# Splitting TensorE sets by columns so that a tile holds 2560 TensorE instructions, with a four-bank first dense layer and gate_w loaded by SyncE

## The chip, the core and the metric

The kernel runs on one core of a Trainium2 chip. The core has a matrix engine (TensorE, PE in the profile; its weight loads are listed as PEld), a vector engine (DVE), a scalar engine (ACT), GpSimd (POOL) and SyncE (SP), which issues most of the transfers, and 16 DMA engines. Every engine works through its own stream of instructions and waits for others by semaphores. The metric is the device time of one execution in microseconds (us); lower is better.

## The reference, cut to what matters

x is [1, 2048, 512]. Branch A walks through 64 segments of 32 tokens; each segment sees 8 memory tokens that the segment before it produced, so the segments form a chain. Branch B is a dense MLP over all 2048 tokens. A gate mixes them.

```python
def _A_ref(x, mem0, Wq, Wk, Wv, Wo, seg_len):      # M = 8, H = 32 heads, Dh = 128
    for s in range(n_seg):                          # 64
        h = concat([mem, x[:, s*32:(s+1)*32]], axis=1)
        q, k, v = h @ Wq, h @ Wk, h @ Wv            # per head
        p = softmax(mask(q @ k.T * Dh ** -0.5))
        o = (p @ v) @ Wo
        mem = o[:, :M]
        outs.append(o[:, M:])
b = gelu(layernorm(x) @ w1 + b1) @ w2 + b2          # 512 -> 1376 -> 512
g = sigmoid((x * gate_w).sum(-1, keepdims=True))
out = g * A(x) + (1 - g) * b
```

## The kernel before, in words

**Stages.** The first part (to about 75 us) computes the MLP. Eight blocks of 256 tokens run through `a_mm` (first dense layer, 11 chunks of up to 128 features; each chunk is four matmuls over 256 columns into a PSUM bank `hp`, then a Gelu on ACT) and `b_mm` (second layer, one matmul of 512 columns for the token tiles that aren't put off). Only even tiles up to 12 get their second layer here, in bank U[0] or U[2]; the hidden values of the others go to DRAM (`h_dr`) and are multiplied later as filler. Meanwhile SyncE loads 16 MB of attention weights. `gate_sums` on DVE multiplies x by `gw_bc`, which is gate_w copied to all 128 partitions.

The second part is the loop over 64 segments (L753 to L866). Four segments are a tile T (128 tokens); `si` is the segment's place in it. A segment does, in the order of the TensorE stream: the q and k projections (`qk_unit`, 64 matmuls of 512 columns), scores, the v projection (`v_unit`), softmax sums, probabilities times v (`av`, L290 and L295: 40 short matmuls), the output projection (`wo_pass`, which calls `wo_group` eight times), and `new_mem`, whose three parts turn the first 8 output rows into the next segment's memory. The chain from one segment to the next goes through `wo_pass`, copies on ACT and `new_mem`.

**Sets of four.** A matmul in this loop fills 32 rows of the output, and four of them stand side by side at column positions 0, 32, 64 and 96 of the array, so they run together. Such a set of four, over 512 columns, is one call of `qk_unit`, `v_unit` or `wo_group`. Every matmul has its own weight load before it, so a set is eight instructions.

**Filler.** `side(T, si)` gives a generator of work that isn't in the chain: projections of tokens left over for the next tile (si 0, 1, 3), `wo_left` for the tile before (si 2). `run(n)` takes n units of it. The lists `WS` say how many units go where: W1 after the v projection, W2 after `av`, W3 after `wo_pass`, then one unit after each of the first two `new_mem` parts. `next(mlp, None)` adds halves of the postponed MLP work.

**What sets the order.** All of it is a hand-written order (`manual_schedule`): each engine's stream is the order in which the Python code emits instructions. The TensorE stream is straight-line code, without loops, up to the rarely taken branch at the end. Counted in it, wait-only instructions included, a tile of the middle of the loop holds 2412 TensorE instructions: segments of 609, 601, 601 and 601.

Of the kernel before, what the change touches and what calls it, by code (L numbers as in the profile page):

```python
# [28 lines left out]
def kernel(ctx, tc, A_x, A_mem0, A_Wq, A_Wk, A_Wv, A_Wo, A_seg_len, B_x, B_w1, B_b1, B_w2, B_b2, gate_w, out):  # L29
    nc = tc.nc  # L30
    P = 128
# [4 lines left out]
    nseg = S // seg  # L36
# [86 lines left out]
    HF = ((0, H // 2), (H // 2, H))  # L123

    def qk_unit(bk, G, t, hf, kc):
        h0, h1 = HF[hf]
        for j in range(4):
            nc.tensor.matmul(bk[32 * j:32 * j + 32, :], lhsT=G[:, kc, :], rhs=W5[t][:, kc, h0:h1, j, :],  # L128
                             start=(kc == 0), stop=(kc == KC - 1), tile_position=(0, 32 * j))

# [14 lines left out]
    def v_unit(bk, G, vb, kc):  # L145
        for j in range(4):
            nc.tensor.matmul(bk[32 * j:32 * j + 32, :], lhsT=G[:, kc, :], rhs=Wv5[:, kc, 4 * vb:4 * vb + 4, j, :],  # L147
                             start=(kc == 0), stop=(kc == KC - 1), tile_position=(0, 32 * j))

# [4 lines left out]

    def wo_group(bk, U_, n):
        j, ih = HORD[n]
        for c in range(4):
            i = 4 * ih + c
            nc.tensor.matmul(bk[32 * c:32 * c + 32, :], lhsT=U_[:, j, i, :], rhs=Wo_sb[:, 4 * i + j, :],  # L159
                             start=(n == 0), stop=(n == NW - 1), tile_position=(0, 32 * c))  # L160

# [139 lines left out]
    with tc.tile_pool(name="mlpw", bufs=1) as mlpw, \  # L301
# [33 lines left out]
        def ld_w2(eng, a, b):  # L335
            eng.dma_start(w2_sb[:, a:b, :], B_w2[a * P:b * P, :].rearrange("(fc p) d -> p fc d", p=P))
# [6 lines left out]
        nc.sync.dma_start(w1_sb[:, :, F1:F], w1v[:, :, F1:F])  # L343
        nc.gpsimd.dma_start(gw_bc[:], gate_w.partition_broadcast(P))
        ld_w2(nc.sync, H2, H2 + 2)
        ld_w2(nc.sync, H2 + 2, FC - 1)
        nc.sync.dma_start(w2_sb[:FR, FC - 1, :], B_w2[(FC - 1) * P:F, :])
        nc.sync.dma_start(w2_sb[FR:FR + 1, FC - 1, :], B_b2.rearrange("(o d) -> o d", o=1))
# [128 lines left out]
        def a_mm(blk, fc):  # L477
            rows = min(P, F - fc * P)
            n = blk * FC + fc
            hp = (SbF, W, U[3], SbF)[n] if n < 4 else (W, SbF, U[2], U[3])[n % 4] if blk == NBLK - 1 else (W, SbF)[n % 2]  # L480
            for kc in range(KC):
                nc.tensor.matmul(hp[:rows, 0:TB * P], lhsT=w1_sb[:, kc, fc * P:fc * P + rows], rhs=yTs[blk][:, kc, :], start=(kc == 0), stop=(kc == KC - 1))  # L482
            nc.scalar.activation(out=hTm[blk % 2][:rows, :, fc, :], in_=hp[:rows, 0:TB * P].rearrange("p (t c) -> p t c", t=TB), func=ACTF.Gelu_apprx_tanh, bias=b1_sb[:rows, fc:fc + 1], scale=1.0)
# [128 lines left out]

    def run(n):
        for _ in range(n):
            next(fill, None)

    def chain(*gens):
# [113 lines left out]

    def wo_pass(U_, cuts=(0, Dm), bk=W):
        for n in range(NW):
            wo_group(bk, U_, n)
        w = cw.tile([P, Dm], BF16, tag="w", bufs=8, name="w")
        for a, b in zip(cuts, cuts[1:]):
            nc.scalar.copy(out=w[:, a:b], in_=bk[:, a:b])  # L737
        return w
# [10 lines left out]


    QK4 = ((0, 0), (1, 0), (0, 1), (1, 1))
    WS = ((2, 2, 1), (2, 2, 2), (2, 2, 2), (2, 2, 2))
    for s in range(nseg):  # L753
# [91 lines left out]
        prep_q(s + 1)  # L845
        w = wo_pass(UT[s % 2], (0, P, 2 * P, Dm), X2)
        if s >= 1:
            ws[s - 1] = w
        run(W3)
        if si:  # L850
# [3 lines left out]
        new_mem(w, hn, 0, si)  # L854
        run(1)
        new_mem(w, hn, 1, si)
        run(1)
        new_mem(w, hn, 2, si)
# [201 lines left out]
```

## Time and profile before

| | |
|---|---|
| median of 3 runs | 754.07 us (753.94 to 754.29) |
| the profiled execution's own time | 755.67 us |
| its span in the profile | 753.8 us |
| TensorE busy | 736.0 us (98%) |
| ScalarE busy | 535.6 us (71%) |
| VectorE busy | 399.5 us (53%) |
| GpSimd busy | 274.2 us (36%) |
| DMA engines busy, first four of 40 slices | 90% or more |
| DMA engines busy after that | 10 to 40% |

The profile has groups of instructions by line (how often, mean time of one, idle time before them and what ended it), a table of waits, the chain of work that ended last, a timeline, and a view of the DMA queues. A wait that is put down to "issue" is time in which an engine waited for nothing that the profile shows. Matmuls are pipelined: a matmul is shown from its start to a modelled end that lies well behind the start of the next, so small gaps between starts do not show as idle time; differences between starts do.

### The profile page before, as it was taken

The numbers are of one execution on the slowest core, as the hardware profiler recorded it, in microseconds if no ns is written. First come the engines' busy times: TensorE is split into PE (matmuls) and PEld (weight loads), VectorE is DVE, ScalarE is ACT, GpSimd is POOL, SyncE is SP. The second block draws the span as 40 slices with busy tenths as digits, with TensorE's granted clock in tenths as the row PEclk, the third lists the DMA queues.
The fourth block names the chain that finished last, engine by engine and source line by source line (L and its number), as shares of the span: only waits on it lengthen the run. The fifth ranks groups of instructions, "written<-read, shape, count | busy, mean of one in ns | idle before, by whom it ended". The sixth has DMA issues, their size and how long they took to land.

```text
span 753.8 us, 45384 instructions
## 1 busy us (share of the span) xinstructions
PE 736.0 (98%) x19896; PEld 429.8 (57%) x19896; DVE 399.5 (53%) x1415; ACT 535.6 (71%) x1627; POOL 274.2 (36%) x516
## 2 busy tenths in 40 slices
PE   8999999999999999999999999999999999999996
PEld 5776555555555555555555565555555655555553
DVE  6776555446454554445554545445464545555444
ACT  5777667777776776777777777767777777777663
POOL 4001323444324444334433344333443334433341
PEclk9999999999999999999999999999999999999999
DMA  9999323122321323221322313231323222222321
GB/s 312 343 335 362 104 85 87 55 76 72 93 77 46 91 70 96 69 83 53 92 77 80 86 46 93 68 96 67 70 72 86 79 72 78 57 90 74 95 70 37
DMA packets 69997, 77.17 MB, mean 102 GB/s; under 512 B 34873, under 2 KB 59938, under 8 KB 68258
## 3 DMA queue, kind: packets, MB, share of 16 engines
q1 hardware_dynamic: 68802, 72.65, 31.4%
q8 instruction: 157, 2.57, 1.4%
q0 software_dynamic: 448, 1.05, 0.5%
q10 hardware_dynamic: 544, 0.52, 0.3%
q14 instruction: 46, 0.38, 0.2%
HBM read 60.21 MB, written 7.70 MB: 90 GB/s over the span
## 4 chain that ended last, share of the span: by engine, by line
PE 91%; DVE 3%; DMA 2%; issue 2%; ACT 1%; POOL 0%; DVEq 0%; SPq 0%; ACTq 0%; POOLq 0%
PE U L128 33%; PE X L159 19%; PE X L147 17%; PE X L128 4%; PE U L290 3%; PE W L674 3%; PE U L147 2%; PE SbF L482 1%; PE U L266 1%; DMA xt<-in_A_x_dram 1%; PE W L482 1%; PE U L489 1%; DVE junk L465 1%; PE SbF L266 1%; PE SbF L701 1%
## 5 line engine op out<-in xcount | busy, mean ns | idle before, releaser
L730 POOL TENSOR_TENSOR UT<-XR,Rb 128x384 bf16<-128x384 bf16 x126 | 140.2, 1134 | 310.1 <-DMA Rb<-r_dr 252.6
L133 ACT CAST Tb<-U 128x512 bf16<-128x512 f32 x288 | 168.7, 586 | 78.7 <-PE U L128 72.5
L128 PEld LDWEIGHTS <-hT 128*32 128x32 bf16 x4096 | 108.9, 96 | 95.5 <-DVE hT L748 1.1
L147 PE MATMUL X<-Wv_sb,hT 128*32 128x512 bf16 x2048 | 144.9, 378 | 0.9 <-issue 0.9
L128 PE MATMUL U<-Wq_sb,hT 128*32 128x512 bf16 x2048 | 145.1, 380 | 0.0
L128 PE MATMUL U<-Wk_sb,hT 128*32 128x512 bf16 x2048 | 144.6, 379 | 0.0
L159 PE MATMUL X<-Wo_sb,UT 128*32 128x512 bf16 x2016 | 123.0, 380 | 0.2
L748 DVE CAST hT<-U 128x8 bf16<-128x8 f32 x126 | 21.0, 167 | 172.0 <-PE U L746 131.1
L811 ACT CAST V<-X 128x256 bf16<-128x256 f32 x256 | 88.7, 372 | 16.4 <-PE X L147 3.5
L137 DVE STREAM_TRANSPOSE QT<-Tb 128x256 f32<-128x256 f32 x128 | 57.0, 446 | 71.9 <-ACT Tb L133 71.5
L159 PEld LDWEIGHTS <-UT 128*32 128x32 bf16 x2048 | 56.6, 96 | 57.1 <-issue 17.7
L707 ACT CAST XR<-U 128x256 bf16<-128x256 f32 x252 | 78.6, 438 | 0.0
L737 ACT CAST w<-X 128x128 bf16<-128x128 f32 x189 | 44.8, 310 | 45.8 <-PE X L159 45.1
L137 DVE STREAM_TRANSPOSE KT<-Tb 128x256 f32<-128x256 f32 x128 | 57.0, 445 | 25.3 <-ACT Tb L133 25.3
L730 POOL TENSOR_TENSOR UL<-XR,Rb 128x128 bf16<-128x128 bf16 x126 | 60.2, 500 | 0.0
L147 PEld LDWEIGHTS <-hT 128*32 128x32 bf16 x2048 | 47.0, 94 | 22.3 <-issue 1.8
L842 ACT CAST UT<-U 128x64 bf16<-128x64 f32 x252 | 35.3, 227 | 28.2 <-PE U L295 28.2
L722 POOL TENSOR_TENSOR racc<-racc,R 128x72 f32<-128x72 f32 x63 | 21.2, 337 | 93.6 <-DVE R L720 49.9
L674 PE MATMUL W<-w_sb,hm 128*32 128x256 bf16 x728 | 52.7, 273 | 0.1
L794 ACT ACTIVATE E<-U 128x64 bf16<-128x64 f32 (+1 forms) x128 | 35.0, 273 | 11.3 <-PE U L270 11.1
L482 PEld LDWEIGHTS <-w_sb 128*128 128x128 bf16 (+1 forms) x352 | 33.5, 100 | 13.4 <-issue 2.4
L159 PE MATMUL X<-Wo_sb,UL 128*32 128x512 bf16 x512 | 39.8, 379 | 0.2 <-issue 0.2
(178 smaller groups left out, 1223.0 us busy)
## 6 DMA issues: line engine op xcount, KB each, us to landing
Rb<-r_dr SPq DMA_DIRECT2D x63, 512.0 KB, 3.9
Wv_sb<-in_A_Wv_dram SPq DMA_DIRECT2D x4, 1024.0 KB, 7.2
Wq_sb<-in_A_Wq_dram SPq DMA_DIRECT2D x4, 1024.0 KB, 8.5
Wk_sb<-in_A_Wk_dram SPq DMA_DIRECT2D x4, 1024.0 KB, 9.0
Wo_sb<-in_A_Wo_dram SPq DMA_DIRECT2D x4, 1024.0 KB, 9.7
VP<-VL SPq DMA_DIRECT2D x64, 64.0 KB, 3.2
hm<-h_dr SPq DMA_DIRECT2D x91, 32.0 KB, 2.2
c<-c_dr SPq DMA_DIRECT2D x16, 128.0 KB, 3.5
```

What stands on the lines that cost most here:

```text
L128: nc.tensor.matmul(bk[32 * j:32 * j + 32, :], lhsT=G[:, kc, :], rhs=W5[t][:, kc, h0:h1, j, :], start=(kc == 0), stop=(kc == KC - 1), tile_ ...
L133: nc.scalar.copy(out=Tb[:], in_=bk.rearrange("p (a b e) -> p a e b", a=8, b=2))
L137: nc.vector.transpose(out=dst[:, 8 * hf:8 * hf + 8, c0:c0 + 32, :].rearrange("p a r b -> p a (r b)").bitcast(FP32), in_=Tb[:].rearrange("p ...
L147: nc.tensor.matmul(bk[32 * j:32 * j + 32, :], lhsT=G[:, kc, :], rhs=Wv5[:, kc, 4 * vb:4 * vb + 4, j, :], start=(kc == 0), stop=(kc == KC - ...
L159: nc.tensor.matmul(bk[32 * c:32 * c + 32, :], lhsT=U_[:, j, i, :], rhs=Wo_sb[:, 4 * i + j, :], start=(n == 0), stop=(n == NW - 1), tile_po ...
L482: nc.tensor.matmul(hp[:rows, 0:TB * P], lhsT=w1_sb[:, kc, fc * P:fc * P + rows], rhs=yTs[blk][:, kc, :], start=(kc == 0), stop=(kc == KC - 1))
L674: nc.tensor.matmul(W[32 * c:32 * c + 32, cc], lhsT=hm[:, 32 * c:32 * c + 32], rhs=w2_sb[:, fc, cc], start=(fc == 0 and h == 0), stop=(fc = ...
L707: nc.scalar.copy(out=XR[:, j], in_=U[j][:, 0:NG * 40].rearrange("p (i q) -> p i q", q=40)[:, :, 0:32])
L730: nc.gpsimd.tensor_tensor(out=out[:, :, 4 * h:4 * h + 4, o:o + b - a], in0=XR[:, :, 4 * h:4 * h + 4, a:b], in1=Rb[:, h, :, :, a:b], op=ALU ...
L737: nc.scalar.copy(out=w[:, a:b], in_=bk[:, a:b])
L811: nc.scalar.copy(out=V[:, i0:i0 + 2, :].rearrange("p i e -> p (i e)"), in_=(X1, X2)[vb][:, 256 * h:256 * h + 256])
L842: nc.scalar.copy(out=UT[s % 2][:, j, :, 0:M], in_=U[j][:, 0:NG * 40].rearrange("p (i q) -> p i q", q=40)[:, :, 32:40])
```

## The change

It does four things.

1. A variable `cut` tells `qk_unit`, `v_unit` and `wo_group` to split each matmul of the set by columns: with `cut[0]` at 2 a set is two rounds of four matmuls over 256 columns, with 4 it is four rounds over 128 columns. Every piece has its own weight load. The computed values are the same.
2. Tables say where this is done. `WHP` and `WH` name the groups of `wo_pass` that are halved, `UCP` and `UC` the cut of the filler units from W3 on. In the tiles 1 to 14 a segment with si 0 gets three halved groups (five in segment 4) and two units in four pieces, a segment with si 2 one half-halved group (`nc4=2`: two of its four matmuls) and three units in four pieces; segment 3 gets two halved groups and two units in four pieces. Tile 15 gets none.
3. `a_mm` takes the banks SbF, W, U[1], U[3] in turn for all chunks, where it took W and SbF in turn (and four banks in the last block).
4. gate_w is loaded by SyncE behind the bulk of w2, where GpSimd's queue loaded it near the start.

```diff
+    cut = [1]
+
     def qk_unit(bk, G, t, hf, kc):
-        h0, h1 = HF[hf]
-        for j in range(4):
-            nc.tensor.matmul(bk[32 * j:32 * j + 32, :], lhsT=G[:, kc, :], rhs=W5[t][:, kc, h0:h1, j, :],
-                             start=(kc == 0), stop=(kc == KC - 1), tile_position=(0, 32 * j))
+        n = H // 2 // cut[0]
+        for a in range(cut[0]):
+            h0 = HF[hf][0] + n * a
+            for j in range(4):
+                nc.tensor.matmul(bk[32 * j:32 * j + 32, 32 * n * a:32 * n * a + 32 * n], lhsT=G[:, kc, :], rhs=W5[t][:, kc, h0:h0 + n, j, :],
+                                 start=(kc == 0), stop=(kc == KC - 1), tile_position=(0, 32 * j))
...
-    def wo_group(bk, U_, n):
+    def wo_group(bk, U_, n, nc4=4):
         j, ih = HORD[n]
-        for c in range(4):
-            i = 4 * ih + c
-            nc.tensor.matmul(bk[32 * c:32 * c + 32, :], lhsT=U_[:, j, i, :], rhs=Wo_sb[:, 4 * i + j, :],
-                             start=(n == 0), stop=(n == NW - 1), tile_position=(0, 32 * c))
+        m = Dm // cut[0]
+        for a in range(cut[0]):
+            for c in range(4 if a == 0 else nc4):
+                i = 4 * ih + c
+                e = slice(m * a, m * a + m) if c < nc4 else slice(0, Dm)
+                nc.tensor.matmul(bk[32 * c:32 * c + 32, e], lhsT=U_[:, j, i, :], rhs=Wo_sb[:, 4 * i + j, e],
+                                 start=(n == 0), stop=(n == NW - 1), tile_position=(0, 32 * c))
...
-        nc.gpsimd.dma_start(gw_bc[:], gate_w.partition_broadcast(P))
         ld_w2(nc.sync, H2, H2 + 2)
         ld_w2(nc.sync, H2 + 2, FC - 1)
+        nc.sync.dma_start(gw_bc[:], gate_w.partition_broadcast(P))
...
-            hp = (SbF, W, U[3], SbF)[n] if n < 4 else (W, SbF, U[2], U[3])[n % 4] if blk == NBLK - 1 else (W, SbF)[n % 2]
+            hp = (SbF, W, U[1], U[3])[n % 4]
...
-    def run(n):
-        for _ in range(n):
+    def run(n, cuts=()):
+        for k in range(n):
+            cut[0] = cuts[k] if cuts else 1
             next(fill, None)
+            cut[0] = 1
...
-    def wo_pass(U_, cuts=(0, Dm), bk=W):
+    def wo_pass(U_, cuts=(0, Dm), bk=W, halves=(), nc4=4):
         for n in range(NW):
-            wo_group(bk, U_, n)
+            cut[0] = 2 if n in halves else 1
+            wo_group(bk, U_, n, nc4 if n in halves else 4)
+            cut[0] = 1
...
+    WHP = (((4, 5, 6),), (), ((6,), 2), ())
+    UCP = ((1, 4, 4), (), (4, 4, 4), ())
+    WH = {3: ((5, 6),), 4: ((2, 3, 4, 5, 6),)}
+    UC = {3: (1, 4, 4)}
...
-        w = wo_pass(UT[s % 2], (0, P, 2 * P, Dm), X2)
+        w = wo_pass(UT[s % 2], (0, P, 2 * P, Dm), X2, *WH.get(s, WHP[si] if 4 <= s < nseg - 4 else ()))
+        uc = iter(UC.get(s, UCP[si] if 4 <= s < nseg - 4 else ()))
...
-        run(W3)
+        run(W3, [next(uc, 1) for _ in range(W3)])
...
-        run(1)
+        run(1, [next(uc, 1)])
         new_mem(w, hn, 1, si)
-        run(1)
+        run(1, [next(uc, 1)])
```

On TensorE, at the end of a segment with si 0 (from tile 2 on), the last group of `wo_pass` is followed by a filler unit, the earlier output's selection, the first part of `new_mem` and the next filler unit. X_123 is the bank X2, UT the attention result, GL the left-over tokens, U_121 the bank U[3]. One pair of each kind stands there before:

```order
L159 LDWEIGHTS UT_1364
L159 MATMUL X_123<-Wo_sb,UT_1364 32x512
...
L128 LDWEIGHTS GL
L128 MATMUL U_121<-Wk_sb,GL 32x512
...
L746 LDWEIGHTS w
L746 MATMUL U_118<-SelM,w 32x8
...
L128 LDWEIGHTS GL
L128 MATMUL U_121<-Wk_sb,GL 32x512
```

and now, with three groups of the pass halved ahead of its last one:

```order
L169 LDWEIGHTS UT_1364
L169 MATMUL X_123<-Wo_sb,UT_1364 32x256
...
L169 LDWEIGHTS UT_1364
L169 MATMUL X_123<-Wo_sb,UT_1364 32x512
L132 LDWEIGHTS GL
L132 MATMUL U_121<-Wk_sb,GL 32x512
...
L760 LDWEIGHTS w
L760 MATMUL U_118<-SelM,w 32x8
...
L132 LDWEIGHTS GL
L132 MATMUL U_121<-Wk_sb,GL 32x128
```

No matmul changed its place; the halved groups hold 16 instructions instead of 8 and the quartered units 32 instead of 8. Segments with si 0 and si 2 grow from 609 and 601 to 681 and 677 instructions, so a tile from tile 1 on holds 681 + 601 + 677 + 601 = 2560.

On SyncE, in the loads at the start, before:

```order
L343 DMA w_sb<-in_B_w_dram 128x4x480
L336 DMA w_sb<-in_B_w_dram 128x2x512 x2
L347 DMA w_sb<-in_B_w_dram 96x512
L348 DMA w_sb<-in_B_b_dram 1x512
L317 DMA xt<-in_A_x_dram 128x512 x2
```

and now:

```order
L353 DMA w_sb<-in_B_w_dram 128x4x480
L346 DMA w_sb<-in_B_w_dram 128x2x512 x2
L356 DMA gw_bc<-in_gate_w_dram 128x512
L357 DMA w_sb<-in_B_w_dram 96x512
L358 DMA w_sb<-in_B_b_dram 1x512
L327 DMA xt<-in_A_x_dram 128x512 x2
```

The load of gate_w (128 KB with its copies) stands behind the two pieces of w2 and ahead of the rest of w2, of b2 and of the next two tiles of x; GpSimd's queue no longer has it.

More of the change, by code (lines that the diff above doesn't have):

```diff
@@ L145, in v_unit @@
     def v_unit(bk, G, vb, kc):
-        for j in range(4):
-            nc.tensor.matmul(bk[32 * j:32 * j + 32, :], lhsT=G[:, kc, :], rhs=Wv5[:, kc, 4 * vb:4 * vb + 4, j, :],
-                             start=(kc == 0), stop=(kc == KC - 1), tile_position=(0, 32 * j))
+        n = 4 // cut[0]
+        for a in range(cut[0]):
+            i0 = 4 * vb + n * a
+            for j in range(4):
+                nc.tensor.matmul(bk[32 * j:32 * j + 32, Dh * n * a:Dh * n * (a + 1)], lhsT=G[:, kc, :], rhs=Wv5[:, kc, i0:i0 + n, j, :],
+                                 start=(kc == 0), stop=(kc == KC - 1), tile_position=(0, 32 * j))
     def v_out(V, vb):
@@ L153 @@
     HORD = [(j, ih) for j in (0, 2, 1, 3) for ih in range(2)]
-    def wo_group(bk, U_, n):
+    def wo_group(bk, U_, n, nc4=4):
         j, ih = HORD[n]
-        for c in range(4):
-            i = 4 * ih + c
-            nc.tensor.matmul(bk[32 * c:32 * c + 32, :], lhsT=U_[:, j, i, :], rhs=Wo_sb[:, 4 * i + j, :],
-                             start=(n == 0), stop=(n == NW - 1), tile_position=(0, 32 * c))
+        m = Dm // cut[0]
+        for a in range(cut[0]):
+            for c in range(4 if a == 0 else nc4):
[3 more added lines that the diff above has]
+                                 start=(n == 0), stop=(n == NW - 1), tile_position=(0, 32 * c))
     NW = len(HORD)
```

## The prediction

> **What bounds the kernel now.** I read the engines' busy times and the chain of work first.
>
> ```profile
> PE 736.0 (98%) x19896; PEld 429.8 (57%) x19896; DVE 399.5 (53%) x1415; ACT 535.6 (71%) x1627; POOL 274.2 (36%) x516
> q8 instruction: 157, 2.57, 1.4%
> PE 91%; DVE 3%; DMA 2%; issue 2%; ACT 1%; POOL 0%; DVEq 0%; SPq 0%; ACTq 0%; POOLq 0%
> ```
>
> TensorE is the bound: 98% busy, 91% of the chain. Only two things can move the end: less work on TensorE, or fewer gaps in it. The second row shows a possible cause of gaps: queue q8 carries instructions, 157 packets of 2.57 MB / 157 = 16.4 KB each. TensorE executes 2 x 19896 = 39,792 instructions; over 157 packets that is 253 each, so a packet is a block of 256 instructions of 64 bytes.
>
> Next, gaps that nothing explains: the waits put down to "issue", and three of them in the timeline.
>
> ```profile
> PE U L290 <- issue: 3.2, 5, 1.0
> PE X L147 <- issue: 1.3, 3, 0.7
> 208.26 0.25 PE L290 MATMUL U<-E,V 32*128 32x40 bf16 x12 [0.69 <-issue]
> 324.25 0.19 PE L290 MATMUL U<-E,V 32*128 32x40 bf16 x1 [0.59 <-issue]
> 501.67 0.22 PE L290 MATMUL U<-E,V 32*128 32x40 bf16 x6 [1.00 <-issue]
> ```
>
> Counted in the order of TensorE's stream, the first instructions after these three gaps are numbers 8898, 15554 and 25794: 26 and 40 blocks of 256 apart, each at 194 beyond a multiple of 256. So TensorE stands still at block boundaries. Was the block late? The DMA view of 499.2 to 500.2 has one packet of q8, and the one from 500.2 to 501.67 has none:
>
> ```profile
> q8 instruction: 1, 0.02, 5.8%
> ```
>
> The block landed by 500.2 and its first instruction ran at 501.67: about 1.47 us from landing to use. A boundary therefore stalls when TensorE arrives earlier than that.
>
> What does it cost in all? A matmul's modelled end hides short gaps, so I compare starts of equal pieces, the first q and k projections of a segment in the chain (x67 rows are segments with si 1, and start some 0.2 us early because filler is merged into them).
>
> ```profile
> 170.12 3.69 PE U L128 x67
> 285.04 3.49 PE U L128 x64
> 296.32 3.68 PE U L128 x67
> 379.31 3.68 PE U L128 x67
> 389.69 3.51 PE U L128 x64
> 441.94 3.51 PE U L128 x64
> 452.14 3.49 PE U L128 x64
> 462.41 3.68 PE U L128 x67
> 599.17 3.49 PE U L128 x64
> 609.35 3.51 PE U L128 x64
> 671.77 3.69 PE U L128 x67
> 170.12:671.77 501.65, 496.65 (x14453) 285.63 (x14448) 256.50 (x907) 364.62 (x1141) 197.49 (x348) 1.00 0.26 76
> 285.04:296.32 11.28, 10.51 (x304) 6.01 (x300) 4.63 (x18) 7.77 (x25) 4.04 (x7) 1.00 0.39 114
> 452.14:462.41 10.27, 10.27 (x304) 5.83 (x300) 4.63 (x18) 7.78 (x25) 4.03 (x7) 1.00 0.44 128
> ```
>
> Twelve tiles take 501.65, or 41.80 each. The two segments in the last rows run the same 304 matmuls at a granted clock of 1.00, one in 11.28, the other in 10.27. From undisturbed segments a tile is 10.27 (si 0, from 452.14) + 10.38 (si 1, from 379.31) + 10.18 (si 2, from 599.17) + 10.20 (si 3, from 441.94) = 41.03. So 0.77 us a tile are lost.
>
> Since a tile holds 2412 = 9 x 256 + 108 instructions, the boundaries wander through the segment from tile to tile. The three gaps above are all in `av`, where 40 short matmuls rush through instructions; boundaries elsewhere often cost nothing.
>
> **The change part by part.** *Fixed boundaries.* With 2560 = 10 x 256 every tile has its boundaries at the same places. Counted in the changed order they stand, from tile 1 on, at instructions 41, 297, 553 of a segment with si 0, at 128 and 384 with si 1, at 39, 295, 551 with si 2, at 130 and 386 with si 3: ahead of or early in `av`, and at the end of `wo_pass` or just after it. The segments that I took as undisturbed had theirs at 26, 282, 538 (si 0), 145, 401 (si 1), 28, 284, 540 (si 2) and 115, 371 (si 3), all within 17 instructions. Tiles 2 to 14, whose phase is new throughout, thus give 13 x 0.77 = 10.0 us if their boundaries cost nothing.
>
> They may not all be free. The halved groups make 553 instructions go by where 529 did, so boundary 553 comes at the end of `wo_pass`, earlier in time than 538 or so did. The block needed there is asked for after boundary 297; its nearest kin are the block after 282 in the segment at 452.14 and the one after 312 in that at 389.69 (si 2). The DMA views of 458.0 to 459.25 and 396.0 to 397.3 show one block each, and the time after them none:
>
> ```profile
> q8 instruction: 1, 0.02, 6.0%
> q8 instruction: 1, 0.02, 5.9%
> 459.34 1.91 PE L159 MATMUL X<-Wo_sb,UT 128*32 128x512 bf16 x32
> 461.06 0.40 PE L128 MATMUL U<-Wk_sb,GL 128*32 128x512 bf16 x4
> 398.65 0.62 PE L159 MATMUL X<-Wo_sb,UL 128*32 128x512 bf16 x8
> ```
>
> First: landed 459.25 + 1.47 = 460.72, needed at the last matmuls of the pass, about 461.0: 0.3 to spare. Second: 397.3 + 1.47 = 398.77, needed 0.1 after 398.65: nothing to spare. Boundaries 297 and 295 lie between these, so each late boundary costs between 0 and, with a block 0.2 later than the second, 0.25; I take 0.1, nearer the first because 282 and 284 are closer to 297 and 295 than 312 is. Two of them and 0.05 for the boundaries at 295 and 297 make 0.25 a tile, 3.25 us over 13 tiles (0 to 7.2).
>
> The Trainium skill, Runtime: NRT & Kernel Launch, section Instruction fetch mechanics, has 16 KiB blocks of 256 instructions too, but calls the cost of crossing one "mostly hidden". The 1.00 us gap above stands against that; by the page nothing would be gained here.
>
> *The pieces.* What a narrower matmul costs shows in the MLP, where every matmul has its own full weight load, and in the pass above:
>
> ```profile
> 21.76 0.39 PE L459 MATMUL X<-ident,y 128*128 128x128 bf16 x4
> 21.98 0.60 PE L482 MATMUL W<-yT,w_sb 128*128 128x256 bf16 x4
> 22.42 0.38 PE L489 MATMUL U<-w_sb,hTm 128*128 128x512 bf16 x1
> L159 PEld LDWEIGHTS <-UT x2048: 92/97/98, 82.0 to 742.8; 128*32 128x32 bf16 x187
> ```
>
> Four of 128 columns take 0.22 us, 55 ns each; four of 256 take 0.44, 110 each; a set of 512 columns takes (461.06 - 459.34) / 8 = 215 ns. A quartered unit is 4 x 55 = 220, 5 more; a halved group 2 x 110 = 220, 5 more as well. Five units and three and a half groups a tile make 0.04 us, 0.5 us in all (0 to 1). They lie on TensorE, so nothing hides them. Weight loads of 97 ns did not hold up the 55 ns matmuls, because they overlap.
>
> The Trainium skill, TensorE: Matmul & The Clock Gate, section Back-to-back issue gap, speaks against this change: in a stream of load and matmul pairs it gives about 81 ns for 128 columns. By that estimate a quartered unit would cost 4 x 81 = 324 ns; the 55 ns of this trace's pairs stands against it.
>
> *Tiles 0, 1 and 15.* Tile 0 keeps its boundaries until segment 3's halved groups, and tile 15 has none of the new pieces; counted there, one boundary falls just behind `av` (456 of segment 61), where before two fell into it (402 of segment 60, 423 of segment 63). I take 0, plus or minus 0.5.
>
> *gate_w and the banks.*
>
> ```profile
> GB/s 312 343 335 362 104 85 87 55 76 72 93 77 46 91 70 96 69 83 53 92 77 80 86 46 93 68 96 67 70 72 86 79 72 78 57 90 74 95 70 37
> 12.47 0.33 PEld L482 LDWEIGHTS <-w_sb 128*128 128x128 bf16 x4 [0.67 <-DMA w_sb<-in_B_w_dram]
> PE SbF L482 <- ACT hTm L483: 0.3, 1, 0.3
> 15.43 0.68 DVE L465 SCALAR_TENSOR_TENSOR junk<-xt,gw_bc 128x512 bf16<-128x512 bf16 x1
> 4.39 2.36 SPq L336 DMA_DIRECT2D w_sb<-in_B_w_dram  x2
> w_sb<-in_B_w_dram SPq DMA_DIRECT2D x2, 256.0 KB, 8.8
> 48.82 8.81 DMA xt<-in_A_x_dram
> ```
>
> At 12.47 TensorE waited 0.67 for w1. Moving 128 KB from ahead of it to behind takes up to 0.4 us (at 312 GB/s, the first slice) off. gate_w would land about 14 to 15 (w2's issues at 4.39 to 6.75, plus 8.8, with transfers abreast), before its first use at 15.43; if it came 0.5 late only DVE would wait, five microseconds ahead of the next transposes. On SyncE it delays two x tiles and w2's last rows by 0.4. Four banks can remove one wait of 0.3 on Gelu. But the last row shows x arriving late at 57.6 with the chain behind it, and that transfer isn't sped up. I take a gain of 0.3 (0 to 0.7).
>
> *The sum.* -10.0 + 3.25 + 0.5 - 0.3 = -6.55. The profiled execution took 755.67 in all (753.8 of span and 1.87 around it), 1.6 more than the median; it becomes 749.1, and the median 754.07 - 6.55 = 747.5.
>
> **The rivals.** *All boundaries free*: the sum without the 3.25 and with the best start is -10.0 + 0.5 - 0.7 = -10.2, 743.9. For it: the undisturbed segments; against: the thin spare at 551 and 553.
>
> *A fixed boundary that is always late*: now a bad phase is bad in all 13 tiles. If the blocks at 551 and 553 come as late as the one at 501.67, each costs 1.00: 13 x 2 - 10.0 + 0.5 = +16.5, 770.6. It turns from gain to loss when the two cost more than 0.77 together, 0.38 each. For it: the spare of 0.3 and 0. Against: it needs blocks some 0.4 later than both measured ones. At 0.3 to 0.38 each the result would be 751.5 to 754, a weak gain or none.
>
> *Weight loads that don't hide in the pieces*: if the four loads of 97 ns in a column position ran in series, a quartered unit would take 388 instead of 215, five of them 0.87 a tile, 11.2 us: 747.5 + 11.2 - 0.3 = 758.4. The 55 ns row speaks against it. By the Trainium skill's 81 ns per matmul (the page named above) the quartered units cost 5 x 109 ns a tile, 7.1 us in all, and it ends at 754.3.
>
> *The change does not do what it says*: the gaps belong to something else at these places, or the boundaries lie elsewhere than I counted. Then only the pieces' cost is left, 754.3. The spacing by multiples of 256 speaks against it.
>
> **How the numbers follow.** The forecast has 0.62; all free 0.13; always late 0.07, and the weak form of it 0.08; exposed loads 0.03 and the skill's spacing 0.02; not doing what it says 0.05. A change below 0.2%, 1.5 us, can't be told from none: faster is below 752.6, slower above 755.6. Faster: 0.62 + 0.13 + 0.03 of the weak form = 0.78. Same: 0.05 + 0.02 + 0.05 = 0.12. Slower: 0.10. The range, 743.8 to 752.4, takes in all boundaries free, and on the other side a residue of 0.6 a tile (-10.0 + 7.8 + 0.5 = -1.7).
>
> **What would show it.** The waits of L290 on issue (3.2 us, 5 times) gone or down to the first and last tiles; tile after tile of nearly equal length, 41.1 to 41.5; TensorE's matmul count up by 1,076 at the same mean times per column; 165 or so packets on q8 (2 x 1,076 / 256 = 8 more). A gap at the end of every `wo_pass` with si 0 and of the units behind it with si 2, each longer than 0.38, would prove me wrong, as would tiles that still differ by a microsecond.

## The result and the profile after

The changed kernel takes 758.95 us (median of 11 runs, 755.56 to 762.49), the one before 754.07 in the same comparison (median of 11, 749.22 to 756.16): a ratio of 1.0071, interval 1.0045 to 1.0097. It is slower. The prediction said 747.5 and gave "slower" a chance of 0.10.

The profiled execution took 757.17 in all, with a span of 755.4. These are the page's rows of the changed kernel that answer to the first three of the prediction: busy time, the instruction queue, the chain.

```profile
PE 736.8 (98%) x20964; PEld 448.6 (59%) x20972; DVE 397.9 (53%) x1415; ACT 535.7 (71%) x1627; POOL 273.8 (36%) x515
q8 instruction: 165, 2.70, 1.5%
PE 92%; DVE 3%; DMA 2%; issue 1%; ACT 1%; SPq 0%; DVEq 0%
```

TensorE is still the bound, with 1,076 more weight loads and 165 blocks on q8, as counted. But its waits on nothing that the profile shows did not go away. In the table of waits (total us, times, longest) `av`'s line, L300 now:

```profile
PE U L300 <- issue: 5.2, 17, 0.6
```

Before it was 3.2 us in 5 gaps of up to 1.0; now there are 17 smaller ones. The chain of the changed kernel gives the starts of segments as before (x67 rows are starts of segments with si 1, here of tiles 3 and 14; x64 rows are starts at other places):

```profile
210.53 3.68 PE U L132 x67
274.17 3.51 PE U L132 x64
284.37 3.49 PE U L132 x64
315.80 3.49 PE U L132 x64
326.60 3.52 PE U L132 x64
674.17 3.68 PE U L132 x67
```

Eleven tiles take 674.17 - 210.53 = 463.64, or 42.15 each, against 41.80 before and 41.32 forecast (41.03 and the 0.29 of the terms). The four rows between are the segments with si 3 of tiles 4 and 5: 10.20 and 10.80 us. The view by windows shows the same 304 matmuls in both, at a granted clock of 1.00:

```profile
274.17:284.37 10.20, 10.20 (x304) 5.74 (x300) 5.28 (x19) 7.58 (x24) 4.32 (x8) 1.00 0.15 45
315.80:326.60 10.80, 10.50 (x304) 5.87 (x300) 4.62 (x18) 7.58 (x24) 4.30 (x8) 1.00 0.23 74
```

Where is the time lost? I summed, over tiles 2 to 14, what each segment takes beyond the shortest of its kind (10.46, 10.18, 10.17 and 10.17 for si 0 to 3 before, 10.48, 10.18, 10.19 and 10.17 now, each from the start of a segment's seventeenth matmul, clear of the merged filler, to that of the next):

| us lost in tiles 2 to 14 | si 0 | si 1 | si 2 | si 3 | sum |
|---|---|---|---|---|---|
| before | 3.5 | 1.7 | 2.1 | 3.1 | 10.5 |
| changed | 1.5 | 6.8 | 0.5 | 4.7 | 13.5 |

So si 0 and si 2 improved, and si 1 and si 3, which hold no piece of the change at all, lose 11.4 us, where they lost 4.9 before (sums of unrounded losses). The block boundaries there are the ones that the prediction put at 128 and 384, 130 and 386 and took as free. From here on a boundary is named by the number of the segment's instructions ahead of it, one less than in the prediction: 127 and 383 with si 1, 129 and 385 with si 3, 552 with si 0, 550 with si 2.

**One late block, followed.** In tile 5, segment with si 3, the timelines of TensorE's weight loads and matmuls show two gaps:

```profile
319.32 0.17 PEld L276 LDWEIGHTS <-KT 128*32 128x32 bf16 x15 [0.33 <-issue]
322.81 0.22 PE L300 MATMUL U<-E,V 32*128 32x40 bf16 x8 [0.27 <-issue]
```

The first is behind the first weight load of the scores (boundary 129), the second in the middle of `av` (boundary 385). In tile 4 neither is there. Ahead of both segments the SyncE queue has the issue of the broadcast of `Rb`, the reciprocals that POOL multiplies the token rows with (L730, 512 KB: 128 packets of 4 KB):

```profile
272.29 0.32 SPq L730 DMA_DIRECT2D Rb<-r_dr  x1
313.83 0.32 SPq L730 DMA_DIRECT2D Rb<-r_dr  x1
```

Relative to the start of the segment that follows they are 1.88 and 1.97 ahead, nearly the same. The first packet of the broadcast starts about 1.0 us after the issue (273.23 and 314.86), in both tiles 0.21 after TensorE passed boundary 550 (273.02 and 314.65). What differs is the block used from 550 on: it had landed 2.42 ahead of that boundary in tile 4 and 2.00 ahead of it in tile 5. The DMA view of tile 4, from 273.0 to 274.7, has the next block (the first 9 in the bar) and the broadcast abreast:

```profile
DMA  0009029209952594999955997977999849935525
q1 hardware_dynamic: 114, 0.44, 70.2%
q8 instruction: 1, 0.02, 5.9%
```

That block started at 273.16, 0.07 ahead of the broadcast, landed at 274.76, and the boundary passed without a gap. In tile 5 the view from 314.75 to 316.9 has 146 packets of q1 and none of q8; the block came in the next one, from 316.9 to 317.9, and the block after it between 320.35 and 321.35:

```profile
q1 hardware_dynamic: 146, 0.51, 73.0%
...
q8 instruction: 1, 0.02, 6.0%
...
q8 instruction: 1, 0.02, 5.9%
```

In the trace the fetch began at 317.01, as the broadcast drained, 2.36 after TensorE had passed boundary 550; it landed at 317.97 and its first instruction ran at 319.32, 1.35 later. The next fetch began at 320.48, 2.51 after that landing, took 0.94, and its code ran at 322.81. So one block delayed by the broadcast makes the next one late too: from use to use 3.49 us, where the 256 instructions between 129 and 385 need 3.1 to 3.25.

**The same over all boundaries** of tiles 2 to 14, counted in the traces. Where no broadcast stands in the way (the trace of `after_nobc`, below) a block starts between 0.84 us before and 1.58 us after TensorE passes the boundary ahead of it, half of them 0.43 to 0.84 after; and in no trace here sooner than 1.9 us after the landing of the block before (2.3 in most). Where TensorE waited, the time from landing to use was 1.2 to 1.6 us (median 1.41). Fetches that began over 1.3 us after the boundary ahead was passed: 47 of 123 before, 46 of 130 now. Gaps over 0.3 us between the starts of neighbouring weight loads at a boundary: 18 before, 35 now. The blocks were late as often as before; the change put TensorE where it needs them.

For the 26 blocks used at 127 and 129 the landing of the block before is what mostly tells them apart. In all 26 TensorE passed the boundary ahead 0.1 to 1.0 us before the first packet of the broadcast, and yet 18 of them began over 1.3 us after that boundary. In these 18 the block before had landed 2.05 to 2.37 us ahead of the broadcast's first packet (2.53 in one), in the other eight 2.33 to 2.73. So a block that may start only some 2.4 us after the landing before it, and then finds the broadcast running, mostly waits until it drains. This is read from one trace; no run here varied it alone.

### The profile page after: what moved, and what is told of

It reads as the page before. It is cut to its first block, busy times and chain, and to the rows that moved or that the text cites. A ratio compares the mean times of both kernels' runs of the same rounds, so it can differ in the third digit from the quotient of the medians.

```text
span 755.4 us, 47527 instructions
## 1 busy us (share of the span) xinstructions
PE 736.8 (98%) x20964; PEld 448.6 (59%) x20972; DVE 397.9 (53%) x1415; ACT 535.7 (71%) x1627; POOL 273.8 (36%) x515
## 3 DMA queue, kind: packets, MB, share of 16 engines
q1 hardware_dynamic: 68946, 72.78, 30.6%
## 4 chain that ended last, share of the span: by engine, by line
PE 92%; DVE 3%; DMA 2%; issue 1%; ACT 1%; SPq 0%; DVEq 0%
PE U L132 33%; PE X L169 18%; PE X L154 16%; PE X L132 4%; PE U L300 3%; PE W L686 3%; PE U L154 2%; DMA xt<-in_A_x_dram 1%; PE U L492 1%; PE U L276 1%; PE SbF L276 1%; PE U L499 1%; PE SbF L492 1%; PE W L492 1%; PE SbF L713 1%
## 5 line engine op out<-in xcount | busy, mean ns | idle before, releaser
L132 PEld LDWEIGHTS <-hT 128*32 128x32 bf16 x4096 | 113.9, 96 | 91.1 <-issue 1.7
L132 PE MATMUL U<-Wk_sb,hT 128*32 128x512 bf16 x2048 | 147.8, 379 | 0.1
L169 PE MATMUL X<-Wo_sb,UT 128*32 128x512 bf16 (+1 forms) x2228 | 121.2, 359 | 0.2 <-issue 0.2
L169 PEld LDWEIGHTS <-UT 128*32 128x32 bf16 x2260 | 61.7, 96 | 54.1 <-issue 11.6
L154 PEld LDWEIGHTS <-hT 128*32 128x32 bf16 x2048 | 50.0, 94 | 18.1
L686 PE MATMUL W<-w_sb,hm 128*32 128x256 bf16 x728 | 51.0, 273 | 0.3 <-issue 0.3
L132 PE MATMUL U<-Wk_sb,GL 128*32 128x512 bf16 (+1 forms) x832 | 39.9, 291 | 0.0
## 6 DMA issues: line engine op xcount, KB each, us to landing
Wo_sb<-in_A_Wo_dram SPq DMA_DIRECT2D x4, 1024.0 KB, 11.4
```

The source lines that it names most:

```text
L132: nc.tensor.matmul(bk[32 * j:32 * j + 32, 32 * n * a:32 * n * a + 32 * n], lhsT=G[:, kc, :], rhs=W5[t][:, kc, h0:h0 + n, j, :], start=(kc ...
L154: nc.tensor.matmul(bk[32 * j:32 * j + 32, Dh * n * a:Dh * n * (a + 1)], lhsT=G[:, kc, :], rhs=Wv5[:, kc, i0:i0 + n, j, :], start=(kc == 0) ...
L169: nc.tensor.matmul(bk[32 * c:32 * c + 32, e], lhsT=U_[:, j, i, :], rhs=Wo_sb[:, 4 * i + j, e], start=(n == 0), stop=(n == NW - 1), tile_po ...
L686: nc.tensor.matmul(W[32 * c:32 * c + 32, cc], lhsT=hm[:, 32 * c:32 * c + 32], rhs=w2_sb[:, fc, cc], start=(fc == 0 and h == 0), stop=(fc = ...
```

## The experiments

The theory at the start: a block asked for when the broadcast is about to run queues behind it, and the floor of about 3.5 us a block (2.5 from landing to the next start, 1 of transfer) carries the delay into the next boundary. Rivals: the two boundaries 3.25 us apart are too close whatever the transfers do; or the loss comes from the loads and banks.

**`pieces_only`: the change without items 3 and 4.**

```diff
-            hp = (SbF, W, U[1], U[3])[n % 4]
+            hp = (SbF, W, U[3], SbF)[n] if n < 4 else (W, SbF, U[2], U[3])[n % 4] if blk == NBLK - 1 else (W, SbF)[n % 2]
+        nc.gpsimd.dma_start(gw_bc[:], gate_w.partition_broadcast(P))
...
-        nc.sync.dma_start(gw_bc[:], gate_w.partition_broadcast(P))
```

> The changed kernel with gate_w back on GpSimd's queue and the old banks in the first dense layer: only the pieces and the new phase of the boundaries are left. Theory (late blocks): the whole loss is in the loop; 1.004 to 1.010 of the kernel before, first segment starting 0.3 us later than in the changed kernel, gaps at boundary 127 to 130 and 383 to 386 of segments with si 1 and 3. Rival (the loads and banks cost): ratio 1.000 or below, as the prediction had it.

760.03 us, ratio to before 1.0087 (1.0058 to 1.0115). The loss is in the loop: in its trace si 1 and si 3 lose 13.1 us in tiles 2 to 14.

**`loads_banks_only`: items 3 and 4 alone** (the kernel before, with the opposite of that diff).

> The kernel before with gate_w on SyncE and four banks in the first dense layer, no pieces. Theory (late blocks): ratio 0.997 to 1.002, the first segment starts about 0.3 us earlier, the loop's stalls stay as scattered as before. Rival (the loads and banks cost): 1.005 or more.

753.19 us, ratio 0.9976 (0.9954 to 0.9998): faster, by 0.2%. The timelines of the kernel before and of this one have the first projections of segment 0 as their first rows on `Wq_sb` and `hT`:

```profile
74.58 0.39 PE L128 MATMUL U<-Wq_sb,hT 128*32 128x512 bf16 x4
```

```profile
73.84 0.39 PE L128 MATMUL U<-Wq_sb,hT 128*32 128x512 bf16 x4
```

The loop starts 0.74 earlier (0.64 in the changed kernel, at 73.94). The rival that these items cost something falls.

**`after_nobc` and `before_nobc`: both kernels without the broadcast** and without the small write to DRAM that feeds it. POOL multiplies with a constant tile, so the normalisation is left out.

```diff
+    Rb1 = lp.tile([P, P, NG], FP32)
+    nc.gpsimd.memset(Rb1[:], 0.03125)
...
-        Rb = cw.tile([P, P, NG], FP32, tag="Rb", bufs=1, name="Rb")
-        nc.sync.dma_start(r_dr[s % 2][:], R[:, 8 * NG:RW])
...
-        nc.sync.dma_start(Rb[:].rearrange("p r e -> p (r e)"), r_dr[s % 2][:].rearrange("r e -> (r e)").partition_broadcast(P))
...
-        Rbs[s] = Rb
+        Rbs[s] = Rb1
```

> The changed kernel without the broadcast of the reciprocals through DRAM: the normalisation of the 32 token rows by their sums is left out, a constant tile takes the place of the 512 KB transfer in each segment. Theory (a block asked for behind the broadcast comes late, and the chain of fetches of 3.5 us each cannot catch up by the next boundary): the next block starts within 1.3 us of the boundary at 550 to 553, lands by 1.5 us into the next segment, the gaps at 127 to 130 and 383 to 386 are gone, tiles of 41.0 to 41.3 us, 742 to 747 us in all. Rival (the boundaries at 128 and 384 are 3.25 us apart and too close whatever the transfers do): the gaps stay, 0.2 to 0.4 us at each 384 or so, 752 us or more.

> The kernel before without the same broadcast (the same part of the normalisation left out). Theory (late blocks): its scattered stalls shrink too, since blocks asked for in the last 2 us of a segment no longer wait; 744 to 749 us. If the broadcast matters for the changed kernel only, 753 to 755.

The changed kernel goes to 743.55 (ratio to before 0.9869, 0.9839 to 0.9899), the one before to 749.16 (0.9929, 0.9903 to 0.9955). In the changed kernel without the broadcast `av`'s wait is nearly gone from the table of waits:

```profile
PE U L300 <- issue: 0.2, 1, 0.2
```

Its chain has these starts of the segments with si 1 of tiles 2 and 14:

```profile
166.77 3.69 PE U L132 x67
...
660.40 3.68 PE U L132 x67
```

And its DMA view from 309 to 313.9, over the start of the segment followed above, has two blocks and nothing else:

```profile
q8 instruction: 2, 0.03, 2.5%
```

Twelve tiles take 493.63, 41.14 each. The block for boundary 129 of tile 5 now started at 310.14, 0.42 after boundary 550 and at nearly the same distance from landing to next start (2.48) as in the trace above, and landed 3.08 ahead of its use; 385 followed without a gap. Boundaries 3.25 us apart are no trouble when the first block is early, so that rival falls. Late starts fell from 46 to 3 of 130, gaps over 0.3 us from 35 to 1; in the kernel before from 47 to 12 of 123, and from 18 to 11. And here the change gives nearly what it was forecast to give: 749.16 - 743.55 = 5.6 us. The 11 gaps that the kernel before keeps without any broadcast, of up to 0.8 us, all stand at boundaries 416 to 489, in `av` or in the filler and the pass right behind it, where TensorE reaches the boundary before the block is ready. So the broadcast is not the only cause there.

**`after_late` and `before_late`: the broadcast later in the segment.** If the broadcast has to run, it might go behind the request.

```diff
+    def bcast(s):
+        Rc = cw.tile([P, NG], FP32, tag="Rc", name="Rc")
+        nc.scalar.copy(out=Rc[:], in_=Rk[0][:, 8 * NG:RW])
+        Rb = cw.tile([P, P, NG], FP32, tag="Rb", bufs=1, name="Rb")
+        nc.sync.dma_start(r_dr[s % 2][:], Rc[:])
+        nc.sync.dma_start(Rb[:].rearrange("p r e -> p (r e)"), r_dr[s % 2][:].rearrange("r e -> (r e)").partition_broadcast(P))
+        Rbs[s] = Rb
...
         for j in range(4):
             nc.scalar.copy(out=XR[:, j], in_=U[j][:, 0:NG * 40].rearrange("p (i q) -> p i q", q=40)[:, :, 0:32])
+            if j == 1:
+                bcast(s)
```

> The changed kernel with the broadcast of R's reciprocals (512 KB, Rb) issued later in the segment: ACT copies the 8 columns to a tile Rc between the copies of the raw token rows, and SyncE's write and broadcast follow from there. Nothing is left out. Theory (a TensorE block asked for after boundaries 550 and 552 queues behind the broadcast, and the floor of 3.5 us a block carries the delay on): the request now goes ahead of the broadcast, the stalls at 127-130 and 383-386 of segments with si 1 and 3 mostly go (11.4 us of tiles 2 to 14 down to under 4), and the time is 744 to 749, not below 743.5, the time without any broadcast. Rival (a broadcast costs some block wherever it stands, or GpSimd gets Rb too late and the last groups of wo_left wait): 754 or more, with the stalls at other boundaries or waits on POOL.

> The same later broadcast in the kernel before. Theory: there the broadcast accounts for about 5 us (754.3 with it, 749.2 without), since its boundaries wander and only some meet it; the later one gives back part: 749 to 753. Rival (the broadcast costs wherever it stands): 754 to 756.

Neither came out as the theory had it. `after_late` took 755.99 (ratio 1.0054, 1.0032 to 1.0075), `before_late` 762.04 (1.0136, 1.0094 to 1.0179). Two rows of `after_late`'s table of waits:

```profile
PE W L686 <- issue: 2.4, 3, 1.2
PE U L300 <- issue: 0.8, 2, 0.5
```

The wait of `av` went from 5.2 to 0.8, as the theory had it, and the loss of si 1 and si 3 from 11.4 to 2.9 us. But a new one stands at L686: boundaries 294 and 296 of si 0 and si 2, whose blocks are asked for where the later broadcast now runs. One such gap in its timeline (tile 6, si 0):

```profile
331.76 0.29 PE L686 MATMUL W<-w_sb,hm 128*32 128x256 bf16 x4 [0.33 <-issue]
```

The DMA view of `after_late` from 328.2 to 330.4 shows the block for it, starting at 328.34 among the broadcast and other loads, and taking until 330.33:

```profile
q1 hardware_dynamic: 418, 0.30, 44.4%
q8 instruction: 1, 0.02, 5.6%
```

Si 0 and si 2 lost 8.7 us in place of 2.0. The delay was moved to another block, which was the rival's forecast. Why `before_late` came out 10 us slower is not settled: between the two profiled executions, whose spans differ by 5.8, tiles 2 to 14 account for 4.0 and what follows them for 2.6.

**`after_plus24`: the phase moved by 24 instructions.**

```diff
-    WH = {3: ((5, 6),), 4: ((2, 3, 4, 5, 6),)}
+    WH = {3: ((5, 6),), 4: ((2, 3, 4, 5, 6),), 5: ((4, 5, 6),)}
```

> The changed kernel with three more halved groups in segment 5 alone (24 instructions once), which moves every later boundary 24 instructions back: 16, 272, 528 with si 0, 103 and 359 with si 1, 14, 270, 526 with si 2, 105 and 361 with si 3. The count of blocks, and 3.25 us between the two boundaries of si 1 and 3, stay. Theory: TensorE reaches the boundary behind av some 0.65 us earlier (three sets of 215 ns), so its request goes ahead of the broadcast in most segments: 745 to 752, and the stalls of si 1 and si 3 down to less than half of 11.4 us. Rival (two boundaries 3.25 us apart are too close under the floor of 3.5 whatever the phase, or 2560 is a bad tile by itself): within 2 us of the changed kernel, 757 to 761.

764.92 us, ratio 1.0167 (1.0138 to 1.0196): the phase matters, but in the wrong direction for the theory's number. The timeline has, for tile 3, the issue of a broadcast at the end of si 2 and the gap that followed in si 3:

```profile
232.17 0.32 SPq L730 DMA_DIRECT2D Rb<-r_dr  x1
...
238.03 0.83 PE L132 MATMUL U<-Wk_sb,hT 128*32 128x512 bf16 x12 [1.09 <-issue]
```

And the DMA views from 233.0 to 235.55 and from there to 236.55:

```profile
q1 hardware_dynamic: 145, 0.53, 69.5%
...
q8 instruction: 1, 0.02, 5.8%
```

TensorE passed boundary 526 at 232.62, earlier in the segment as forecast. But the block for it had landed only at 230.91, and 230.91 + 2.5 = 233.4 is just behind the start of the broadcast (233.13). So the next fetch started at 235.67, and TensorE reached boundary 105 sooner than it had reached 129: 1.48 between the starts of two weight loads. My expectation had let the request follow the boundary alone; where blocks follow each other this closely, it follows the landing of the block before.

**`after_bf16`: half the bytes.**

```diff
-    r_dr = [dram.tile([P, NG], FP32, name=f"r_dr{i}") for i in range(2)]
+    r_dr = [dram.tile([P, NG], BF16, name=f"r_dr{i}") for i in range(2)]
...
-        Rb = cw.tile([P, P, NG], FP32, tag="Rb", bufs=1, name="Rb")
-        nc.sync.dma_start(r_dr[s % 2][:], R[:, 8 * NG:RW])
+        Rb = cw.tile([P, P, NG], BF16, tag="Rb", bufs=1, name="Rb")
+        Rh = cw.tile([P, NG], BF16, tag="Rh", name="Rh")
+        nc.vector.tensor_copy(out=Rh[:], in_=R[:, 8 * NG:RW])
+        nc.sync.dma_start(r_dr[s % 2][:], Rh[:])
```

> The changed kernel with the reciprocals broadcast in bf16, 256 KB for 512 (one more rounding of them, and one small cast on DVE). Theory: the queue ahead of the late block is half as long, about 1.1 us for 2.2; a block held up by 1.1 is late by little, so a good part of the 13.6 us of stalls goes: 747 to 754. Rival (what counts is that the broadcast comes ahead at all, not its length, for instance since a queue is served only when another is empty or the floor of 3.5 us alone makes the stall): 757 to 760.

772.53 us (762.3 to 774.92), ratio 1.0205 (1.0117 to 1.0293): slower than either expected, by how much is unsure, since four runs scatter over 12 us. The page's rows of q1, of the changed kernel and of this one:

```profile
q1 hardware_dynamic: 68946, 72.78, 30.6%
```

```profile
q1 hardware_dynamic: 68946, 56.13, 27.3%
```

The packets stayed at 68,946, so 23% fewer bytes saved 9% of the time (27.3% of the span of 770.6 against 30.6% of 755.4); a broadcast went from 2.5 to 2.0 us from its first packet to its last (medians), not to half. That alone explains a small gain at best. It does not explain the loss: gaps of up to 1.7 us at boundaries 38, 40, 127 and 129. Six of 130 blocks took over 2 us to arrive, which none did in the changed kernel. Nor are blocks the whole of it. The table of TensorE's waits has a row that the changed kernel's lacks, two waits for loads of `hm` ahead of tile 2:

```profile
PE W L686 <- DMA hm<-h_dr: 3.6, 2, 2.2
```

Of the 15.2 us between the two spans 6.5 lie ahead of tile 2, and 8.4 in tiles 2 to 14. Why is open: the cast on DVE, the smaller write and the smaller packets were not tried apart.

**`after_mix`: the later place in si 0 and si 2 alone.** The two traces, changed and late, are good in different halves: with the old place si 0 and si 2 lose 2.0 us, with the later one si 1 and si 3 lose 2.9. The broadcast issued in si 0 and si 2 runs at the start of si 1 and si 3. So it goes late in si 0 and si 2 alone, one ACT copy earlier than in `after_late`. `bcast` is here the write to DRAM, and `bcast2` the broadcast.

```diff
         for j in range(4):
+            if j == 1 and s % 2 == 0:
+                Rc = cw.tile([P, NG], FP32, tag="Rc", name="Rc")
+                nc.scalar.copy(out=Rc[:], in_=Rk[0][:, 8 * NG:RW])
+                bcast(s, Rc[:])
+                bcast2(s)
...
+        if s % 2:
+            bcast(s, R[:, 8 * NG:RW])
         hm_load(owed[0])
         owed[0] = 0
+        if s % 2:
+            bcast2(s)
```

> The changed kernel with the later broadcast in segments with si 0 and 2 alone (from Rc, between the copies of the raw token rows), and the old place in segments with si 1 and 3. Nothing is left out. Theory (each block is asked for at a place in the tile that the boundaries fix; a broadcast costs where it meets such a request): the broadcast of si 0 and 2, which in the changed kernel held up the blocks used at 127-130 of si 1 and 3, goes behind that request as in after_late, and that of si 1 and 3, which in after_late held up the blocks used at 294 and 296, stays where it met none. So the stalls of tiles 2 to 14 are the sum of the good halves of the two traces, about 2.2 us for si 0 and 2 and 2.9 for si 1 and 3, 5 us against 13.6: 748 to 753, faster than both kernels. Rival (the fetches run at their floor of 3.5 us nearly all the time, so that a broadcast costs some block wherever it stands): 754 to 759, with the stalls at other boundaries.

749.79 us (747.94 to 751.5), ratio 0.9937 (0.9914 to 0.996): as expected, and faster than both kernels. `av`'s wait in its table of waits:

```profile
PE U L300 <- issue: 1.0, 2, 0.5
```

The last work ahead of tiles 2 and 14 in its timeline:

```profile
158.57 0.20 PE L776 MATMUL SbF<-SelM,w 128*32 128x8 bf16 x8
...
655.37 0.20 PE L776 MATMUL SbF<-SelM,w 128*32 128x8 bf16 x8
```

Twelve tiles take 496.80, 41.40 each. In tile 5, si 3, the DMA view from 312.8 to 314.45 shows the order reversed; the lone block is the 9 in the bar, the broadcast what follows it:

```profile
DMA  0000000000090000000000000000995084440928
q1 hardware_dynamic: 23, 0.09, 22.4%
q8 instruction: 1, 0.02, 4.6%
```

The broadcasts of si 1 and si 3 did not stay where they ran, though the code leaves their issue in place. Measured from the start of the next segment, the first packets of all four came later than in the changed kernel, by 0.9, 1.4, 1.0 and 0.6 us for si 0 to 3 (medians of 13). And they still meet requests: 24 blocks began over 1.3 us after the boundary ahead, and 19 of these are the ones for 294 and 296, which the broadcasts of si 1 and si 3 now delay. They cost little here (six gaps over 0.3 us); the blocks for 127 and 129, on which the changed kernel lost most, came ahead of the broadcast in 25 of 26 cases and abreast of it in one.

**`after_shift`: the phase moved by 128.**

```diff
-    WH = {3: ((5, 6),), 4: ((2, 3, 4, 5, 6),)}
-    UC = {3: (1, 4, 4)}
+    WH = {3: ((5, 6),), 4: ((2, 3, 4, 5, 6),), 5: ((1, 2, 3, 4, 5, 6),), 7: ((3, 4, 5, 6),)}
+    UC = {3: (1, 4, 4), 5: (1, 4, 4, 1)}
```

> The changed kernel with 128 more instructions once (six halved groups and two quartered units in segment 5, four halved groups in segment 7): from tile 2 on the boundaries stand at 168, 424, 680 with si 0, at 255 and 511 with si 1, at 166 and 422 with si 2, at 1, 257 and 513 with si 3. Theory: the boundaries 424, 422, 511 and 513 lie in av or at its end, where the kernel before lost 0.8 to 1.2 us (417 to 457, si 0), 0.03 to 0.4 (419 to 459, si 2), 0 to 0.2 (508 to 520, si 1) and 0.3 to 0.4 (490 to 518, si 3); the sum of 1.1 to 1.9 a tile over 13 tiles, 14 to 25 us, takes the place of the changed kernel's 13.6: 758 to 769. Rival (the count of 2560 matters and the phase does not): 757 to 761 with the stalls still at the start of si 1 and 3.

782.84 us, ratio 1.0355 (1.0313 to 1.0397): the direction as expected, the size beyond it. Two rows of its table of waits:

```profile
PE U L300 <- issue: 9.3, 16, 1.3
PE U L132 <- issue: 8.9, 13, 2.2
```

And two gaps of its timeline, in tile 6 with si 0:

```profile
345.66 0.22 PE L300 MATMUL U<-E,V 32*128 32x40 bf16 x8 [0.99 <-issue]
...
350.77 0.38 PE L132 MATMUL U<-Wk_sb,GL 128*32 128x512 bf16 x1 [1.14 <-issue]
```

The stalls in `av` are those that the kernel before had there. The last row is boundary 680, behind the split pieces; its block started at 348.47, 2.8 us after the boundary in `av`, within the broadcast (347.13 to 350.66). It stalled in all thirteen tiles, with 0.4 us and more between two starts, and is what the expectation lacked, which summed the boundaries in and behind `av` alone. Segments with si 0 alone lost 20.9 us.

The losses of tiles 2 to 14 in one table, as above, each kernel with pieces against the shortest segments of the changed one, the others against those of the kernel before:

| us lost | si 0 | si 1 | si 2 | si 3 | sum | gaps over 0.3 us |
|---|---|---|---|---|---|---|
| before | 3.5 | 1.7 | 2.1 | 3.1 | 10.5 | 18 |
| before without broadcast | 2.7 | 1.2 | 1.6 | 0.2 | 5.7 | 11 |
| changed | 1.5 | 6.8 | 0.5 | 4.7 | 13.5 | 35 |
| changed without broadcast | 0.6 | 0.3 | 0.5 | 0.2 | 1.5 | 1 |
| `after_late` | 4.4 | 1.1 | 4.3 | 1.9 | 11.6 | 22 |
| `after_plus24` | 3.9 | 4.7 | 3.2 | 7.7 | 19.5 | 26 |
| `after_shift` | 20.9 | 2.8 | 11.4 | 1.8 | 37.0 | 51 |
| `after_mix` | 1.7 | 0.4 | 1.4 | 1.2 | 4.8 | 9 |

## Why the prediction was wrong

*What bounds the kernel, and what the gaps are.* Right: blocks of 256 instructions on q8, 165 of them now, with about 1.4 us from landing to use.

*The loss of 0.77 us a tile.* Right in size as a loss, and fixed boundaries can take it away: the kernel before lost 10.5 us in tiles 2 to 14, and without the broadcast the change gains 5.6 us of the 6.55 forecast. About 5 of the 10.5 us, though, were the broadcast's (10.5 - 5.7), and a fixed phase takes those away only where it keeps the blocks clear of it.

*The boundaries at 128, 130, 384 and 386 taken as free.* This is the step that failed. It rested on the nearness of places: undisturbed segments "had theirs at" 115, 371, 145 and 401, "all within 17 instructions". What makes a block late is not where it is used but when it can start, and that depends on the boundary ahead, on the landing of the block before, and on what the DMA engines carry then. Ahead of 145 the boundary lay 256 unsplit instructions back, at 498 of a segment of 609, which was passed some 8.2 us into it and 1.1 ahead of the broadcast; even so its block (at 378.13 in that trace) started only 0.07 ahead of the broadcast. Ahead of 127 and 129 the boundary now lies behind the split groups, at 552 and 550, 8.9 and 9.2 us into the segment, 0.4 to 0.9 and 0.1 to 0.4 ahead of the broadcast (1.05 in one tile); with 2.3 us and more to wait from the landing before, 18 of the 26 blocks came too late to go first. The pieces have their share in it: they pack 72 more instructions into the end of si 0, so that 256 instructions back from 128 reach to 552, where without them it would be 481, at the start of `wo_pass`. The step was worth 0 in the sum and cost 11.4 us in 13 tiles.

*The boundaries at 295, 297, 551 and 553.* Priced at 0.25 a tile, 3.25 us; si 0 and si 2 lost 2.0 in all. Right, within the bounds, but I looked for the late block at its end (the last matmuls of `wo_pass`) and not at the request that leaves from there.

*The rival "a fixed boundary that is always late"* was the mechanism, at another place: not 551 and 553 but the next ones on, and at 0.2 to 0.8 us rather than 1.00. Its turning point, 0.77 a tile, was passed: 11.4 / 13 = 0.88 in si 1 and si 3, and 0.16 in the others.

*The pieces.* Right. The shortest segments of the four kinds add up to 40.98 before and 41.01 now, 0.03 against the 0.04 a tile that was forecast. The timeline of the changed kernel, tile 5, has two quartered units and the next work:

```profile
314.54 0.63 PE L169 MATMUL X<-Wo_sb,UL 128*32 128x128 bf16 x32
314.98 0.29 PE L686 MATMUL W<-w_sb,hm 128*32 128x256 bf16 x4
```

Eight rounds of four in 0.44 us are 55 ns each, the price taken from the MLP. The Trainium skill's 81 ns (TensorE: Matmul & The Clock Gate, section Back-to-back issue gap) is not what this kernel shows.

*gate_w and the banks.* Taken as 0.3 of 0 to 0.7; the loop starts 0.64 earlier in the changed kernel, 0.74 with these items alone, whose runs gain 0.24% (0.02 to 0.46%). The upper end.

*The sum.* Forecast for tiles 2 to 14: -10.0 + 3.25 + 0.5 = -6.25. Measured between the two profiled executions: 543.25 to 546.56, +3.3. With the start's -0.64 and about -1.1 in the other tiles that is the +1.6 between the spans, 753.8 and 755.4. The medians differ by 4.9: the profiled execution of the changed kernel is at the fast end of its runs, which scatter over 7 us.

## What to carry to other kernels

In a long straight-line stream like this one, instruction blocks are transfers with a schedule of their own: work out when each can start, not only where it is used, and see what the DMA engines carry at that time. Fixing the places of the boundaries makes what happens there happen in tile after tile. Here that lost 0.7% with the broadcasts where they were, and gained 0.6% with them 0.6 to 1.4 us later. A stall that a neighbouring position does not have is no evidence for a new position whose predecessor has moved.

## What the runs showed of the hardware

- Blocks have a rate. From the landing of one to the start of the next there were at least 2.3 us in nearly all cases, about 1 us of transfer, and 1.2 to 1.6 from landing to the first instruction of a late one; a chain of late blocks advances by 3.5 us a block (317.01 to 320.48 above). An undisturbed tile has 41.01 / 10 = 4.1 us for each. Why the 2.3 us pass is not shown.
- One block of 16 KB waits behind a 512 KB broadcast on another queue: in tile 5 it started only as 128 packets of 4 KB drained, 2.36 us after the boundary ahead. It does not always wait for all of it: the block at 328.34 in `after_late` started amid the packets and took 1.99 us, where 1.0 is the median. The Trainium skill, Runtime: NRT & Kernel Launch, section Instruction fetch mechanics, calls the crossing of a block "mostly hidden"; the trace agrees for the changed kernel without the broadcast (1 gap over 0.3 us at 130 boundaries) and not for the one with it (35), nor quite for the kernel before without it (11 at 123).
- Half the bytes in as many packets took four fifths of the time: 128 packets of 4 KB took 2.5 us, 128 of 2 KB took 2.0.
- Moving the phase of the stream by 24 or 128 instructions, with TensorE's work unchanged but for some narrower pieces, changed the time by 1% and 3% (ratios 1.0167 and 1.0355 against 1.0071).
